# A group norm kernel on one core: longer runs of loads and stores, and more of the sum on TensorE

## The chip, the cores and the metric

The kernel runs on one core of one Trainium2 chip. The metric is the device time of one execution in microseconds (us). A trace of one execution gives the times of each instruction, of each DMA packet, and of each increment that a finished DMA makes on its semaphore.

Engines: PE is TensorE (matmul), DVE is VectorE, ACT is ScalarE, POOL is GpSimd, SP is SyncE, which here only issues the DMAs. A letter q behind a name (SPq) is the engine's sequencer. L129 is line 129 of the kernel.

## The reference

`x` has the shape (128, 1024, 32, 16) in bf16. Each sample has 32 groups of 32 channels; a group is normalized by its own mean and variance, then each channel is scaled and shifted.

```python
def reference(x, g, b):
    xr = x.reshape(B, 32, C // 32, H, W)
    mu = xr.mean(axis=(2, 3, 4), keepdims=True)
    var = ((xr - mu) ** 2).mean(axis=(2, 3, 4), keepdims=True)
    xn = (xr - mu) / jnp.sqrt(var + 1e-5)
    return xn.reshape(B, C, H, W) * g[None, :, None, None] + b[None, :, None, None]
```

## The kernel before

Four samples make a tile: 128 partitions (sample, group) of F = 16384 columns, 4 MB. There are NT = 32 tiles and a ring of 6 slots. A tile is loaded, normalized in place and stored from the same slot.

```python
SLOTS = 6
RUNS = (2, 3, 3, 3, 3, 3, 3, 3, 3, 6)   # stores issued in a row; then as many loads
NQ = 4
PE_CHUNKS = 12                          # chunks of 512 columns that TensorE sums
PAIRED = F - PE_CHUNKS * MM_FREE        # columns that VectorE sums
# ... cut ...
    def store_parts(i):
        return NQ if i == NT - 1 else 1         # the last store in quarters

    def on_sync(e):
        def load(j):
            if j >= SLOTS:
                e.wait_ge(st[j % SLOTS], 16 * (j // SLOTS))     # slot stored?
            e.dma_start(out=slot(j), in_=x_v[j]).then_inc(ld[j % SLOTS], 16)

        def store(i):
            w = F // store_parts(i)
            for p in range(store_parts(i)):
                e.wait_ge(done, NQ * i + NQ // store_parts(i) * (p + 1))
                e.dma_start(out=..., in_=...).then_inc(st[...] or s_fin, 16)

        for j in range(SLOTS):
            load(j)
        i = 0
        for run in RUNS:
            for n in range(run):
                store(i + n)
            i += run
            for j in range(i + SLOTS - run, min(i + SLOTS, NT)):
                load(j)
        e.wait_ge(s_fin, 16 * sum(store_parts(i) for i in range(NT - SLOTS, NT)))
```

For the mean of a tile TensorE adds 12 chunks through an identity matrix into PSUM, and VectorE adds the other 10240 columns as pairs of 5120 (`pair`, tile name jp). ScalarE then reads the mean (jm), takes the squares in two halves (ja), and the standard deviation. VectorE applies 32 `tensor_scalar` instructions to the tile, one per channel (tile name ring).

## Time and profile before

| | before |
|---|---|
| time, median of 3 runs | 632.13 us (631.5 to 632.31) |
| bytes moved | 268.4 MB, half in, half out |
| DMA queue busy | 99.1% of 16 engines' span |
| VectorE / ScalarE / TensorE busy | 84% / 80% / 25% |
| a 32 KB packet on one DMA engine | 1.213 us (median) |

From the page of the kernel before: the mean busy share of the 16 DMA engines in 40 equal slices of the span (in tenths), what they moved, and the data queue with packets, MB and share.

```profile
DMA  8999999999999999999999999999999999999996
GB/s 366 432 432 409 434 436 432 432 434 434 428 432 432 432 434 430 434 430 432 432 432 428 432 432 432 432 432 432 432 432 432 432 426 432 430 430 436 432 421 271
...
q1 hardware_dynamic: 9648, 268.44, 99.1%
```

The rate is flat: most slices are at 428 to 436 GB/s, with the queue busy 99.1%. So the bytes set the time, and what can still be won lies at the start and in the last slice with its 271 GB/s.

The end in stretches of 2 us (kernel before). The columns are: from and to, length, busy time and count of PE, PEld, DVE, ACT and POOL, granted PE clock, mean busy share of the 16 DMA engines, GB/s.

```profile
620.00:622.00 2.00, 0.00 (x0) 0.00 (x0) 0.22 (x1) 0.00 (x0) 0.00 (x0) 0.50 1.09 455
622.00:624.00 2.00, 0.00 (x0) 0.00 (x0) 0.00 (x0) 0.00 (x0) 0.00 (x0) 0.50 0.95 397
624.00:626.00 2.00, 0.00 (x0) 0.00 (x0) 0.00 (x0) 0.00 (x0) 0.00 (x0) 0.50 0.35 147
626.00:628.00 2.00, 0.00 (x0) 0.00 (x0) 0.00 (x0) 0.00 (x0) 0.00 (x0) 0.50 0.19 82
628.00:630.00 2.00, 0.00 (x0) 0.00 (x0) 0.00 (x0) 0.00 (x0) 0.00 (x0) 0.50 0.04 16
```

Read the share as a number of engines: one engine alone is 1/16 = 0.06. All engines are busy until 624 us; then 0.35 (five or six engines), 0.19 (three), and the last packet ends at 628.9 us. The computation was over at 620.2. So the kernel ends some 5 us after most DMA engines are through, because a few of them are late.

How late each one is can be read all along. The trace before has 16 separate increments for each of its 69 DMAs (1104 in all). I read them as the landings of the 16 engines' shares. The spread of a DMA's 16 landings is how far the last engine is behind the first; below it is called the lag. The kernel before, in us; "2nd" is the lag of the last but one:

```
DMA (first landing)   load 12.8   load 51.6   load 207.3   load 333.3   load 449.4   load 565.7   store 604.3
lag of the last          0.78        0.79         2.44         3.58         4.25         5.16        5.45
lag of the 2nd           0.44        0.45         1.40         3.27         4.09         4.98        5.22
```

The groups of the computation that the change touches (kernel before): line, engine, operation, tiles, shapes, count | busy us, mean ns | idle before, and who ended it.

```profile
L287 DVE TENSOR_SCALAR ring<-ring,scl,bia x1024 | 333.7, 413 | 1.2
L254 DVE SCALAR_TENSOR_TENSOR jp<-ring 128x5120 fp8e5 (+1 forms) x32 | 175.8, 5493 | 60.7 <-PE ps L178 48.7 <-issue 12.0
L178 PE MATMUL ps<-ring,eye 128*128 128x512 bf16 x384 | 156.5, 581 | 424.9 <-DVE jp L254 292.5 <-DMA ring<-in_x_dram 132.5
```

And a piece of the timeline in the first 200 us, when six tiles lie ready and compute runs back to back (start, length, engine, line, operation):

```profile
105.14 0.20 DVE L275 RECIPROCAL rstd<-std 128x1 f32 x1
...
106.03 10.43 DVE L287 TENSOR_SCALAR ring<-ring,scl,bia  x32
...
116.96 5.49 DVE L254 SCALAR_TENSOR_TENSOR jp<-ring 128x5120 fp8e5 x1 [0.50 <-issue]
...
122.38 0.20 DVE L275 RECIPROCAL rstd<-std 128x1 f32 x1
```

From one reciprocal to the next is 17.24 us, and VectorE does not rest. The first loads land 9.71 us apart (12.77 and 22.48 us), so a tile's load and store take 2 x 9.7 = 19.4 us of DMA, and in the long run compute, at 17.24 us, is the quicker of the two.

### The profile page before, as it was taken

Reading aid. Unit: us, or ns where it says so; the run is one execution under the profiler, and the core shown is the slowest. Engines: PE = TensorE matmul, PEld = TensorE weight load, DVE = VectorE, ACT = ScalarE, POOL = GpSimd, SP = SyncE. Lnnn points to the kernel's source line nnn. Section 1 sums busy time; section 2 is a strip of 40 time slices with the busy share of each in tenths; the row PEclk is TensorE's granted clock in tenths of the full one; section 3 lists DMA queues with packets and bytes.
Section 4 is the critical chain, followed back from the end, with each engine's and each line's share of the span. In section 5 each row is a group of like instructions: output and inputs, shape, how many; then the busy total and the mean of one; then the engine's idle time right before and its main releaser. Section 6 shows DMA issues by size and latency. Waiting matters only on the chain.

```text
span 630.7 us, 2595 instructions
## 1 busy us (share of the span) xinstructions
PE 156.7 (25%) x385; PEld 0.2 (0%) x2; DVE 529.6 (84%) x1185; ACT 504.0 (80%) x258; POOL 1.0 (0%) x8
## 2 busy tenths in 40 slices
PE   1433333212223220332053014202220430053000
PEld 0000000000000000000000000000000000000000
DVE  1669999999999999699789959995998699599963
ACT  0798999999999999689948977894999499859960
POOL 0000000000000000000000000000000000000000
PEclk9766655566665765666566557656665665565555
DMA  8999999999999999999999999999999999999996
GB/s 366 432 432 409 434 436 432 432 434 434 428 432 432 432 434 430 434 430 432 432 432 428 432 432 432 432 432 432 432 432 432 432 426 432 430 430 436 432 421 271
DMA packets 9745, 268.45 MB, mean 426 GB/s; under 512 B 1168, under 2 KB 1168, under 8 KB 1168
## 3 DMA queue, kind: packets, MB, share of 16 engines
q1 hardware_dynamic: 9648, 268.44, 99.1%
q10 hardware_dynamic: 96, 0.00, 0.0%
q14 instruction: 1, 0.01, 0.0%
HBM read 134.22 MB, written 134.22 MB: 426 GB/s over the span
## 4 chain that ended last, share of the span: by engine, by line
DMA 44%; ACT 40%; DVE 7%; issue 4%; PE 2%; DVEq 2%; SPq 0%
ACT ja L224 37%; DMA out_dram<-ring 28%; DMA ring<-in_x_dram 16%; DVE ring L287 6%; PE ps L178 2%; ACT jm L216 2%; DVEq L270 1%; ACT var L234 1%; ACT std L238 1%; DVE jp L254 1%; DVEq L273 0%; DVE bia L281 0%; DVE scl L277 0%; DVEq L275 0%; DVEq L254 0%
## 5 line engine op out<-in xcount | busy, mean ns | idle before, releaser
L224 ACT ACTIVATE ja<-ring,nm 128x8192 fp8e5<-128x8192 bf16 x64 | 455.8, 7122 | 2.1
L287 DVE TENSOR_SCALAR ring<-ring,scl,bia x1024 | 333.7, 413 | 1.2
L178 PE MATMUL ps<-ring,eye 128*128 128x512 bf16 x384 | 156.5, 581 | 424.9 <-DVE jp L254 292.5
L254 DVE SCALAR_TENSOR_TENSOR jp<-ring 128x5120 fp8e5 (+1 forms) x32 | 175.8, 5493 | 60.7 <-PE ps L178 48.7
L216 ACT ACTIVATE jm<-ps 128x513 fp8e5<-128x513 f32 x32 | 19.2, 602 | 98.7 <-PE ps L178 98.7
L275 DVE RECIPROCAL rstd<-std 128x1 f32 x32 | 6.3, 198 | 11.9 <-ACT std L238 11.9
L224 ACT ACTIVATION_READ_ACCUMULATOR ja<-ring,nm 128x1 f32 x64 | 11.9, 186 | 0.0
L281 DVE SCALAR_TENSOR_TENSOR bia<-scl,nm,gb 128x32 f32<-128x32 f32 x32 | 8.0, 251 | 4.2
L238 ACT ACTIVATE std<-sq,var 128x1 f32<-128x1 f32 x32 | 9.4, 294 | 1.0
L234 ACT ACTIVATE var<-sq,eps_t 128x1 f32<-128x1 f32 x32 | 9.4, 294 | 1.0
L266 DVE COPY gb<-gb_p 128x64 f32<-128x64 f32 x1 | 0.2, 225 | 11.5 <-PE gb_p L173 11.5
L277 DVE TENSOR_SCALAR scl<-gb,rstd 128x32 f32<-128x32 f32 x32 | 7.7, 241 | 1.1
L216 ACT ACTIVATION_READ_ACCUMULATOR jm<-ps 128x1 f32 x32 | 6.2, 194 | 0.0
L254 DVE DVE_READ_ACCUMULATOR jp<-ring (+1 forms) x32 | 4.5, 142 | 0.0
L173 PE MATMUL gb_p<-gb_b,rep 32*128 32x64 bf16 x1 | 0.2, 205 | 11.3 <-DMA gb_b<-in_b_dram 11.3
L212 ACT ACT_TABLE_LOAD x1 | 1.3, 1283 | 1.9 <-issue 1.9
L155 POOL TENSOR_SCALAR_AFFINE_SELECT rep<-ones_b 32x128 bf16<-32x128 bf16 x1 | 0.3, 303 | 0.0
L151 POOL TENSOR_SCALAR_AFFINE_SELECT eye<-ones_b 128x128 bf16<-128x128 bf16 x1 | 0.3, 293 | 0.4 <-issue 0.4
L212 ACT ACTIVATE warm<-eps_t 128x1 f32<-128x1 f32 x1 | 0.2, 203 | 0.0
L145 POOL MEMSET ones_b<- 128x128 bf16 x1 | 0.2, 205 | 0.5 <-SPq L294 0.5
L175 PEld LDWEIGHTS <-eye 128*128 128x128 bf16 x1 | 0.1, 105 | 0.1
L173 PEld LDWEIGHTS gb_p<-gb_b,rep 32*128 32x128 bf16 x1 | 0.1, 100 | 11.3 <-issue 11.3
(5 smaller groups left out, 0.5 us busy)
## 6 DMA issues: line engine op xcount, KB each, us to landing
ring<-in_x_dram SPq DMA_DIRECT2D x32, 4096.0 KB, 29.1
out_dram<-ring SPq DMA_DIRECT2D x31, 4096.0 KB, 31.3
out_dram<-ring SPq DMA_DIRECT2D x4, 1024.0 KB, 7.0
gb_b<-in_g_dram ACTq DMA_DIRECT2D x1, 2.0 KB, 6.5
gb_b<-in_b_dram ACTq DMA_DIRECT2D x1, 2.0 KB, 9.7
```

The source lines that it names most:

```text
L178: return e.add_instruction(mybir.InstMatmult(name=nc.get_next_instruction_name(), engine=e.engine, start_tensor_calc=(k == 0), stop_tensor ...
L212: e.activation(out=warm[:], in_=eps_t[:], func=ACT.Sqrt)
L216: e.activation(out=jm[:], in_=sums_and_pairs(c), func=ACT.Identity, scale=-inv_n, accum_out=nm[:, c : c + 1], saturate=False,).then_inc(me ...
L224: e.activation(out=ja[:], in_=slot(c)[:, h * (F // 2) : (h + 1) * (F // 2)], func=ACT.Square, bias=nm[:, c : c + 1], scale=1.0, accum_out= ...
L234: e.activation(out=var[:], in_=sq[:, 0:1], func=ACT.Identity, bias=eps_t[:], scale=inv_n).then_inc(varred[c], 1)
L238: e.activation(out=std[:, c : c + 1], in_=sq[:, 1:2], func=ACT.Sqrt, bias=var[:], scale=inv_n).then_inc(stded, 1)
L254: e.scalar_tensor_tensor(out=jp[:], in0=part(i, lo, n), scalar=1.0, in1=part(i, lo + n, n), op0=ALU.mult, op1=ALU.add, accum_out=ps[:, bas ...
L270: e.drain()
L275: e.reciprocal(out=rstd[:], in_=std[:, bass.ds(i % SLOTS, 1)]).then_inc(inverted, 1)
L277: e.tensor_scalar(out=scl[:], in0=gb[:, 0:KC], scalar1=rstd[:], scalar2=None, op0=ALU.mult).then_inc(scaled, 1)
L281: e.scalar_tensor_tensor(out=bia[:], in0=scl[:], scalar=nm[:, bass.ds(i % SLOTS, 1)], in1=gb[:, KC : 2 * KC], op0=ALU.mult, op1=ALU.add,). ...
L287: ts = e.tensor_scalar(out=a, in0=a, scalar1=scl[:, k : k + 1], scalar2=bia[:, k : k + 1], op0=ALU.mult, op1=ALU.add,)
```

## The change

Its intent: longer runs, so that the DMA queue changes between loads and stores less often (eight runs instead of ten). Longer runs need tiles earlier, so VectorE's share of the sum is cut by a fifth and given to TensorE, and the third store goes in halves, since its second half is not ready when the queue would run dry. Last, a semaphore increment is put behind the final wait.

```diff
-RUNS = (2, 3, 3, 3, 3, 3, 3, 3, 3, 6)
+RUNS = (3, 4, 4, 4, 4, 4, 3, 6)
-PE_CHUNKS = 12
+PE_CHUNKS = 16
 # ... cut ...
     def store_parts(i):
-        return NQ if i == NT - 1 else 1
+        return {2: 2, NT - 1: NQ}.get(i, 1)
 # ... cut ...
             if j >= SLOTS:
-                e.wait_ge(st[j % SLOTS], 16 * (j // SLOTS))
+                e.wait_ge(
+                    st[j % SLOTS], 16 * sum(store_parts(i) for i in range(j % SLOTS, j, SLOTS))
+                )
 # ... cut ...
         e.wait_ge(s_fin, 16 * sum(store_parts(i) for i in range(NT - SLOTS, NT)))
+        e.sem_inc(s_end, 1)
```

More of the change, by code (lines that the diff above doesn't have):

```diff
@@ L102 @@
     first_in, paired, stded, done = (sem(n) for n in ("first", "pair", "std", "done"))
-    s_gb, s_ones, s_eye, s_gbp, s_fin = (
-        sem(n) for n in ("gbl", "ones", "eye", "gbp", "fin")
+    s_gb, s_ones, s_eye, s_gbp, s_fin, s_end = (
+        sem(n) for n in ("gbl", "ones", "eye", "gbp", "fin", "end")
     )
     def store_parts(i):
-        return NQ if i == NT - 1 else 1
+        return {2: 2, NT - 1: NQ}.get(i, 1)
     def slot(i):
```

## The prediction

The trace before shows one clear dip, 360 GB/s from 58 to 62 us, and the slices at the other nine changes are at 426 to 432. The sum came to 632.1 - 0.9 = 631.2 us; item 1 is its only term. The 0.43 us of a matmul in item 2 is that of the trace before (12 in 5.17 us at 53.62 us).

> What bounds the kernel now. Each tile is 4 MB in and 4 MB out, 268.4 MB in all. The page's slices show 430 to 436 GB/s almost everywhere; the queue table has the DMA engines busy 99.1%. [...] So DMA is the limit, though the chain that ended last names ACT for 40%. In the packet records a 32 KB packet takes 1.213 us (median); 512 per engine are 621.1 us, from the first packet at 2.0. That ends at 623.1. Most of the 16 engines do end near 624, but the last at 628.9, without a gap before: they lag. [...] First-to-last spread of one DMA's 16 landings: 0.8 us for the first load, 1.25 after the first change from loads to stores, 3.1 at 275 us, 5.0 at 507, 5.45 at 604. It grows almost only where stores follow loads (ten times: 60, 100, 158, 217, 275, 333, 391, 449, 507, 565 us), 0.44 us each on average[...]. That lag is the tail: the last slice moves 271 GB/s.
>
> What the change does.
> 1. Eight runs, not ten: two load-to-store changes fewer. Estimate: 2 x 0.44 = 0.9 us less lag on the last engine, directly on the critical path. This is the main term.
> 2. VectorE pairs 4096 columns rather than 5120: at 5.49 us for 5120, about 4.40, so 1.1 us less per tile. Where compute runs back to back (52 to 219 us in the chain) the period is 17.24 us and VectorE never rests; I expect about 16.5, as ScalarE's 15.8 to 15.9 plus hand-over then also limits. TensorE gets 4 x 0.43 = 1.7 us more per tile, hidden, except behind a fresh load. DMA needs 19.4 us per tile, so this buys nothing in the middle; it permits longer runs. I reckon tile 2's first half ready at 75 us (the queue empties at about 81) and tile 6 at 146.5, the queue empty at about 149; with 17.24 per tile it would be 151. A short shortage starves only the leading engines, which have over 4 us in hand.
> 3. Tile 31 is finished about 3 us earlier (now 620.2), and the leading engines' gap of 0.2 to 0.4 us at 604 goes. Neither touches the lagging engines: no gain.
> 4. Store 2 in halves: 16 KB packets. From 8 KB packets (0.309 us, 1.236 per 32 KB) under 0.1 us.
> 5. The last wait is now carried by a branch at 629.35, next instruction 0.155 us later. On an increment: within 0.1 us either way.
>
> Sum: 632.1 - 0.9 = 631.2 us; range 630.2 to 632.1. Chances: faster by over 2% 0.005, within 2% 0.985, slower 0.01.
>
> What would show it. Landing spread at the last whole-tile stores about 4.5 us, not 5.45; last packet about 628, leading engines still near 624; [...]pairing about 4.4 us; period about 16.5; no gap near 149 us; tile 31 done near 617.
>
> What would make it wrong. The growth may depend on bytes, or on how far apart the engines already are, not on the number of changes: then nothing is gained. Longer runs may make each change dearer. Tile 6 may come later than 149 us by more than the lag, and the whole queue stops. The before runs scatter by 0.8 us, about the size of the effect.

## The result

| | before | after |
|---|---|---|
| time, median of 4 runs each | 632.22 us (631.5 to 632.48) | 632.59 us (632.04 to 633.41) |
| ratio, fast runs | | 1.0009 (95%: 0.9991 to 1.0026) |
| instructions in the trace | 2595 | 2719 |
| tile 31 finished | 620.2 us | 617.4 us |
| last packet ends | 628.89 us | 628.91 us |
| lag at the last whole store | 5.45 us | 5.21 us |
| lag of the 2nd there | 5.22 us | 0.66 us |

A ratio is the mean time of one kernel's fast runs over that of the other's of the same rounds, so it is not quite the ratio of the medians quoted. The two kernels can't be told apart. The forecast of 0.9 us less did not come, and 632.59 us lies outside the range.

The page of the kernel after, same lines:

```profile
DMA  8999999999999999999999999999999999999995
GB/s 366 432 432 422 434 428 438 434 434 432 432 432 432 432 430 432 432 432 432 432 432 432 430 432 432 432 432 432 432 432 432 432 434 434 436 424 436 434 423 243
```

The end of the kernel after, in the same stretches:

```profile
620.00:622.00 2.00, 0.00 (x0) 0.00 (x0) 0.00 (x0) 0.00 (x0) 0.00 (x0) 0.50 1.03 434
622.00:624.00 2.00, 0.00 (x0) 0.00 (x0) 0.00 (x0) 0.00 (x0) 0.00 (x0) 0.50 0.92 389
624.00:626.00 2.00, 0.00 (x0) 0.00 (x0) 0.00 (x0) 0.00 (x0) 0.00 (x0) 0.50 0.09 37
626.00:628.00 2.00, 0.00 (x0) 0.00 (x0) 0.00 (x0) 0.00 (x0) 0.00 (x0) 0.50 0.07 29
628.00:630.00 2.00, 0.00 (x0) 0.00 (x0) 0.00 (x0) 0.00 (x0) 0.00 (x0) 0.50 0.02 8
```

This is the surprise. Where 0.35 and 0.19 stood, there is now 0.09 and 0.07: one engine of the sixteen. Fifteen engines are through together, and one still ends at 628.9 us. In this trace the lags of all but one engine stay at about 0.7 us or less up to the last whole store, and that one is as late as before. Its landings show how it gets there: the lag of the last engine (us) at the load just before and just behind each run of stores, with the loads' first landings.

```
run of stores           129-159         207-237         285-314         362-392         440-469         517-537
load before, lag      120.2  0.57     197.6  1.56     275.1  2.81     352.7  3.27     430.3  3.79     507.7  4.35
load behind, lag      168.5  1.33     246.0  2.21     323.5  3.38     401.2  3.81     478.6  4.36     546.4  4.81
```

I had assumed that it jumps where stores follow loads. Two such jumps are there (0.2 us at 198, 0.6 at 275), but the rest is creeping: over every run of four stores it loses 0.5 to 0.8 us (0.46 over the last run, of three), and over most groups of loads nothing.

The computation did what it was meant to do. The groups and the timeline after:

```profile
L290 DVE TENSOR_SCALAR ring<-ring,scl,bia x1024 | 333.7, 420 | 1.2
L181 PE MATMUL ps<-ring,eye 128*128 128x512 bf16 x507 | 185.0, 537 | 393.8 <-DVE jp L257 239.0 <-DMA ring<-in_x_dram 153.6 <-issue 1.1
L257 DVE SCALAR_TENSOR_TENSOR jp<-ring 128x4096 fp8e5 (+1 forms) x32 | 141.6, 4425 | 83.3 <-PE ps L181 71.3 <-issue 12.0
```

```profile
117.70 0.17 DVE L278 RECIPROCAL rstd<-std 128x1 f32 x1
...
118.57 10.43 DVE L290 TENSOR_SCALAR ring<-ring,scl,bia  x32
...
129.49 4.42 DVE L257 SCALAR_TENSOR_TENSOR jp<-ring 128x4096 fp8e5 x1 [0.49 <-issue]
...
134.46 0.16 DVE L278 RECIPROCAL rstd<-std 128x1 f32 x1 [0.48 <-ACT std L241]
```

The pairing takes 4.43 us for 5.49, and the period alternates between 16.16 and 16.77 us (in the second VectorE waits 0.48 us for ScalarE), 16.46 on average for 17.24.

### The profile page after: what moved, and what is told of

The parts are those of the page before. It is cut to its first block, busy times and chain, and to the rows that moved or that the text cites. A ratio compares the mean times of both kernels' runs of the same rounds, so it can differ in the third digit from the quotient of the medians.

```text
span 631.0 us, 2719 instructions
## 1 busy us (share of the span) xinstructions
PE 185.2 (29%) x508; PEld 0.2 (0%) x2; DVE 497.4 (79%) x1185; ACT 504.0 (80%) x258; POOL 1.0 (0%) x8
## 4 chain that ended last, share of the span: by engine, by line
ACT 37%; DMA 23%; DVE 22%; issue 8%; PE 4%; DVEq 3%; SPq 0%; ACTq 0%
ACT ja L227 34%; DMA ring<-in_x_dram 23%; DVE ring L290 20%; PE ps L181 4%; ACT jm L219 2%; DVEq L273 1%; DVEq L276 1%; ACT var L237 1%; DVE jp L257 1%; ACT std L241 1%; DVE bia L284 1%; DVE scl L280 1%; DVEq L257 0%; DVE rstd L278 0%; SPq L131 0%
## 5 line engine op out<-in xcount | busy, mean ns | idle before, releaser
L290 DVE TENSOR_SCALAR ring<-ring,scl,bia x1024 | 333.7, 420 | 1.2
L181 PE MATMUL ps<-ring,eye 128*128 128x512 bf16 x507 | 185.0, 537 | 393.8 <-DVE jp L257 239.0
L257 DVE SCALAR_TENSOR_TENSOR jp<-ring 128x4096 fp8e5 (+1 forms) x32 | 141.6, 4425 | 83.3 <-PE ps L181 71.3
L176 PE MATMUL gb_p<-gb_b,rep 32*128 32x64 bf16 x1 | 0.2, 208 | 11.1 <-DMA gb_b<-in_b_dram 11.1
```

The costliest lines, as they stand in the source:

```text
L181: return e.add_instruction(mybir.InstMatmult(name=nc.get_next_instruction_name(), engine=e.engine, start_tensor_calc=(k == 0), stop_tensor ...
L257: e.scalar_tensor_tensor(out=jp[:], in0=part(i, lo, n), scalar=1.0, in1=part(i, lo + n, n), op0=ALU.mult, op1=ALU.add, accum_out=ps[:, bas ...
L290: ts = e.tensor_scalar(out=a, in0=a, scalar1=scl[:, k : k + 1], scalar2=bia[:, k : k + 1], op0=ALU.mult, op1=ALU.add,)
```

## The experiments

Two theories stood against each other, and a third came up on the way.

- Theory A: one DMA engine loses a little in every store, whatever the runs are. It ends last in both kernels. The changes from loads to stores delay other engines, which in the kernel before happened to end up about as late as that one, so that the trace before could not tell the two causes apart. The change removed, at most, the lateness that did not count.
- Rival B: my prediction, that lateness comes from the changes alone.
- Rival C: the single late engine of the trace after was chance.

About the cause of the creeping: rival D says that the compute engines' traffic in SBUF delays it; theory A1 says that executed instructions do, by themselves.

### b_probe and a_probe: which engine is late

Each kernel with 16 tiny loads queued behind the last store:

```diff
+        for k in range(16, 0, -1):
+            e.dma_start(
+                out=probe[0:k, k * 16 - 16 : k * 16], in_=x_v[0][0:k, 0:16]
+            ).then_inc(s_probe[k - 1], 16)
```

The probe of 5 partitions has 5 landings in the traces, beside one earlier step of its semaphore for the rest of the 16. A late engine is named here by the smallest probe in which its late landing shows, less one: if it shows with 5 partitions and not with 4, it is engine 4. The traces give no numbers of engines, so this is a name; that it stands for one and the same engine in all probes and all runs is my assumption and was not shown.

> The kernel before, with 16 tiny loads queued behind the last store: the k-th names k partitions (k = 16 down to 1)[...]. Theory A (one engine loses about 0.14 us in every 4 MB store, whatever the runs; the changes from loads to stores cost other engines time, but not beyond what that one loses anyway): the last landing is about 5.2 us behind the first, one engine's lag grows by 0.12 to 0.16 us per store inside the runs of stores, some others grow at the changes. Rival B (my prediction: only the changes cost): the late engines lose only at the ten changes, about 0.44 us each.

> The changed kernel with the same 16 probes. Theory A: again exactly one engine 4.5 to 5.5 us late, all others under 1.5 us, and the same engine number as the one in the kernel before whose lag grows in stores. Rival B: the late engine differs from run to run and loses at the eight changes only. Rival C (the single late engine was chance): several engines late, as in the trace before.

Both results were correct (one look each; 634.99 and 634.98 us, with the probes' own time at the end). The latest landing of each probe, in us of the span:

```
partitions    16     15     14     13     12     11     10      9      8      7      6      5      4
b_probe     629.6  629.9  630.1  630.3  630.5  630.7  630.9  631.0  631.2  631.4  631.6  631.8  629.6
a_probe     629.9  630.1  630.2  630.4  630.6  630.8  631.0  631.2  631.4  631.6  631.8  631.9  627.7
```

In both kernels the late landing is there down to 5 partitions (631.8 and 631.9 us) and gone at 4 (629.6 and 627.7): it is engine 4. It was 4.9 us behind in b_probe and 5.0 in a_probe at the last whole store. Its lag grew by 0.35 to 0.42 us over each run of three stores (b_probe, from 159 us on). That supports theory A. What I had expected of a_probe beside it failed: two more engines were 4.0 and 2.5 us late there (engines 13 and 15, named in the same way), and three others in b_probe (15 at 3.4, 14 and 11 at 2.6). So the tidy picture of the trace after was in part chance (a grain of rival C), but engine 4 is the last one in both probed traces and the others come second.

### dma_only: the same bytes without computation

```diff
-        on_gpsimd(nc.gpsimd)
-        on_tensor(nc.tensor)
-        on_scalar(nc.scalar)
-        on_vector(nc.vector)
```

SP issues 32 loads, waits for them, and issues 32 stores (then the probes).

> No computation (a wrong result on purpose): 32 loads into the ring, then 32 stores from it, one change only, then the probes. Theory A: spread of landings stays under 1 us through the loads, grows by about 0.14 us per store after that, in one engine, to about 4.5 to 5 us at the end; time about 2 + 621 + 5 + 2 = 630 us. Rival B (only changes cost): spread under 1.3 us at the end, time about 626 us. Rival D (VectorE or TensorE traffic on SBUF delays that engine): no growth here either, about 626 us.

No engine fell behind: 0.6 us through the loads (the spread of the start), 0.2 us from the first store to the one at 568.6 us. After that one engine was 0.7 to 0.9 us late; that is when SP issued the probes (556 to 588 us), and by the probes it is engine 4 again. The time, 633.25 us, shows no gain: the probes at the end landed up to 629.9 us, and SP waits for all loads before the first store. In dma_tiny, with the same DMAs, the page's slice at that place (304 to 321 us) moved 372 GB/s between slices of 434, by my estimate 16.9 us x (1 - 372/434), some 2.4 us of DMA time. Theory A in its first form is wrong: engine 4 is not slow in stores as such. Something that the computation does makes it slow.

### dma_sbuf and dma_sbuf2: traffic in SBUF without many instructions

```diff
+    def big_v(e):
+        with nc.Fori(0, 11, 1, engines=[e.engine]):
+            for _ in range(10):
+                e.tensor_scalar(out=out_v, in0=src, scalar1=1.0, scalar2=0.0, ...)   # 128 x 8192
+                e.drain()
+    # the same on ScalarE: 80 activations of 128 x 8192
```

Loads and stores go through four slots; VectorE and ScalarE work in the other two. Wrong result on purpose.

> Loads, then stores, through four slots of the ring (a wrong result on purpose), beside some 110 long VectorE and 80 long ScalarE instructions that read and write the other two slots: much traffic in SBUF, few instructions. Rival D: engine 4 falls behind by about 0.14 us per store, 4 to 5 us at the end. Theory A1: under 0.5 us, since there are only about 400 instructions in place of 2600.

The lag stayed at 0.24 us or less to 568.8 us. But VectorE's instructions took 2.29 us each and were over at 273 us, before the stores began, so this said something of ScalarE only. dma_sbuf2 repeats it with VectorE's loop of 130 behind the last load:

> As dma_sbuf, where VectorE had ended before the stores began; here its 130 long instructions (2.3 us each) start with the stores, beside ScalarE's. Rival D (traffic in SBUF delays the late engine): 0.1 us per store or more, 3 us or more behind at 568 us. Theory A1 (executed instructions do): under 0.5 us there.

Two stretches of the stores in dma_sbuf2 (no TensorE here: busy time and count of DVE, ACT and POOL, granted clock, DMA share, GB/s):

```profile
325.00:569.00 244.00, 233.55 (x103) 241.04 (x38) 0.00 (x0) 1.00 1.00 432
569.00:627.00 58.00, 54.46 (x24) 20.09 (x3) 0.00 (x0) 1.00 0.99 425
```

VectorE was busy 96% and ScalarE 99% of the 244 us in which 25 stores ran, more than in the real kernel (84% and 80%), and the lag at 568.5 us was 0.22 us, as without any computation. Rival D is out for these operations (TensorE's reads were not tried).

### dma_tiny: many instructions without traffic

A drain, as written here, names no tile: it has no operand to read or write. The page of dma_tiny counts 7344 instructions.

```diff
+    def tiny(e):                      # on VectorE
+        e.wait_ge(ld[(NT - 1) % SLOTS], ...)     # behind the last load
+        with nc.Fori(0, 400, 1, engines=[e.engine]):
+            for _ in range(16):
+                e.drain()
```

> Loads, then stores, no computation (a wrong result on purpose), and 6400 empty instructions (drains) on VectorE that start with the stores: many instructions, no traffic in SBUF. Theory A1[...]: one engine falls behind by several us while the drains run. Rival D (traffic of the compute engines in SBUF delays it): spread stays under 0.3 us, as without computation.

The lag grew from 0.33 us at the first store to 11.1 at 568.6 us and 14.5 at the last, 0.43 us in each store; every other engine stayed within 0.24 us. By the probes it is engine 4 (on another chip than b_probe and a_probe: 8, not 3). (The kernel's own 677.69 us are the drains', which went on until 675 us.) The end of the DMA in dma_tiny (POOL, clock, DMA share, GB/s):

```profile
325.00:569.00 244.00, 0.00 (x0) 1.00 1.01 431
569.00:627.00 58.00, 0.00 (x0) 1.00 0.99 424
627.00:641.00 14.00, 0.00 (x0) 1.00 0.06 23
```

A share of 0.06 for 14 us is one engine of sixteen, alone. In dma_only nothing moves after 627 us:

```profile
569.00:627.00 58.00, 0.00 (x0) 1.00 0.99 425
627.00:630.00 3.00, 0.00 (x0) 1.00 0.00 0
```

So instructions without operands delay engine 4, and only it (14.5 us, all others within 0.24). More packets of kind "instruction" are not the reason: the pages of dma_tiny and dma_only both count one. Theory A1 is shown for this artificial case.

### drains: the same in the real kernel

```diff
+        tiny(nc.gpsimd)       # 6400 drains on the idle GpSimd, from the first load on
```

The 2.4 ns of this expectation and of the next is an estimate from dma_tiny: 0.43 us per store over some 177 drains per store (6400 drains in about 350 us, 9.7 us a store).

> The changed kernel with 6400 empty instructions (drains) on the idle GpSimd from the first load on. Theory A1 (engine 4 is delayed by about 2.4 ns for each instruction that any engine executes while it stores; from 0.43 us per store at about 177 drains per store): if the drains last about 400 us, half of them meet stores: 3200 x 2.4 ns = 7.7 us more, 640 us, ratio 1.012, engine 4 alone some 13 us behind. If instructions don't matter beside computation: 632.6, ratio 1.000.

641.8 us (641.13 to 642.1), ratio 1.015 (1.0135 to 1.0166), a correct result. The last engine has no probes here and is taken for engine 4. Its lag grew by 1.9 to 2.0 us over each run of four stores between 120 and 352 us, where it grows by 0.55 to 0.65 without drains; over the loads between it stood still (3.70 us at 168 us, 3.67 at 198), and at 608 us it was 9.8. The drains ended at 493 us, but from about 390 us on the lag hardly grew any more: a load waits for all 16 landings of a store, so the other engines ran out of work and waited for engine 4 (the last whole store's first landing came at 608.4 us instead of 604.6). The kernel lost 9 us (641.8 for after_again's 632.77 in the same rounds) to an engine, GpSimd, that had nothing to do with the computation.

### few_instr: fewer instructions in the real kernel

```diff
-            for k, a in enumerate(parts):                      # 32 x 512 columns
+            for q in range(NQ):                                # 4 x 4096 columns
+                k, a = q * KQ, part(i, q * KQ * HW, KQ * HW)
                 ts = e.tensor_scalar(out=a, in0=a, scalar1=scl[:, k : k + 1], ...)
-                if (k + 1) % KQ == 0:
-                    ts.then_inc(done, 1)
+                ts.then_inc(done, 1)
```

> The changed kernel with the normalization in 4 instructions of 4096 columns a tile in place of 32 of 512 (a wrong result on purpose: one channel's factors for eight): 896 instructions fewer, of 2719, the same traffic. Theory A1 (engine 4 loses about 2.4 ns for each instruction executed while it stores): 896 / 2 x 2.4 ns = 1.1 us less lag, about 0.09 us per store where it was 0.13, 3.7 to 4.2 us at the last whole stores; time 631.3 to 631.7 us, ratio to before 0.998 to 0.999. If the lag in the real kernel comes from something else: 0.13 us per store, about 5 us, 632.6 us.

631.19 us (630.59 to 631.52), ratio to before 0.998 (0.9967 to 0.9994): faster by 0.4 to 2.1 us, where 1 us was expected. (The changed kernel was not timed in these rounds; split_only, with the same division of the sums, took 632.54.) The last packet ended at 627.4 us instead of 628.9. The page's first line, and the group of the normalization:

```profile
span 629.5 us, 1823 instructions
```

```profile
L291 DVE TENSOR_SCALAR ring<-ring,scl,bia x128 | 163.7, 1342 | 1.2
```

VectorE's busy time fell too (163.7 for 333.7 us), so the instructions are not the only difference; but in dma_sbuf2, with VectorE busy 96%, the lag stayed at 0.22 us. The lag of the last engine at the last whole store was 3.85 us; the next engine, 3.49.

Put side by side, the lag that the last engine gains in the middle of the kernel:

| kernel | instructions begun per 9.7 us | lag per store, us |
|---|---|---|
| dma_only / dma_sbuf2 | 1 / 13 | 0.00 / 0.00 |
| few_instr | 27 | 0.08 (0.32 to 0.36 per four) |
| b_probe (before's computation) | 40 | 0.13 (0.35 to 0.42 per three) |
| after, after_again | 41 | 0.14 to 0.16 (0.54 to 0.66 per four) |
| drains | 186 | 0.49 (1.94 to 2.04 per four, to 352 us) |
| dma_tiny | 195 | 0.43 |

The first column counts the instructions in the trace in the same stretch. Early stretches are left out in which another engine was last, so few_instr counts from 198 us on and b_probe from 159. By an estimate from the two columns it is roughly 2 to 4 ns for each instruction, and nothing at 13 per store; so it is no strict proportion, but the order is clear.

### runs_of_2: more changes between loads and stores

```diff
-RUNS = (2, 3, 3, 3, 3, 3, 3, 3, 3, 6)
+RUNS = (2, 2, 2, 2, 2, 2, 2, 2, 2, 2, 2, 2, 2, 6)
```

> The kernel before with runs of two (thirteen twos, then six): 14 changes from loads to stores instead of 10, all else as before. Rival B (my prediction, 0.44 us per change on the engine that ends last): 1.8 us slower, 634.0 us, ratio 1.0028. Theory A (engine 4 ends last because it loses about 0.13 us per store; the changes delay other engines, 0.33 us each on the worst): the worst other engine goes from about 3.4 to 4.7 us behind, still in front of engine 4 at 5; time within 0.5 us of before, ratio 0.999 to 1.001.

633.05 us (632.72 to 633.45), ratio 1.0014 (1.0000 to 1.0027). That is 0.9 us, between the two expectations: by this estimate four more changes cost 0.2 us each, half of what I had predicted, but the interval runs from 0 to 1.7 us and so all but reaches both expectations. The trace has the latest two engines at 6.3 and 5.9 us at the last whole store; one of them still grows by 0.1 us per store in the last six (6.00, 6.11, 6.19, 6.29), as engine 4 does, and the other stands still (5.9). So with 14 changes another engine has caught up with the one that ends last; that the changes cost the kernel time is likely, and not clear of the noise.

### split_only, runs_only and after_again: the parts of the change

split_only is the kernel before with 16 chunks on TensorE and the final increment; runs_only is the kernel before with the new runs and the halved third store; after_again is the changed kernel once more.

```diff
 # split_only                                  # runs_only
-PE_CHUNKS = 12                               -RUNS = (2, 3, 3, 3, 3, 3, 3, 3, 3, 6)
+PE_CHUNKS = 16                               +RUNS = (3, 4, 4, 4, 4, 4, 3, 6), store 2 in halves
```

> The kernel before with the new division of the sums (16 chunks on TensorE) and the increment after the last wait; the runs stay ten and the third store whole. Theory A: 632.0 to 632.7 us, ratio 0.999 to 1.001, engine 4 about 5 us behind, no starving: the quicker computation is worth nothing by itself. If it is worth something: below 631.5.

> The kernel before with the new runs and the halved third store alone; the division of the sums between TensorE and VectorE stays (12 chunks). Prediction's reckoning: tile 6 is ready at about 151 us while the leading engines run dry at about 149; they starve 1 to 3 us, and the engine that ends last is only 1 us behind by then, so the end moves by 0.5 to 2 us: 633 to 634.5 us. If the longer runs needed no faster computation: 632.2, ratio 1.000.

> The changed kernel unchanged, for the same chip as the others and as a second trace. Theory A: 632.2 to 632.9 us, ratio 1.000 to 1.001; one engine 4.7 to 5.3 us behind at the last whole stores.

| | us, median of 5 | ratio to before (95%) |
|---|---|---|
| split_only | 632.54 | 1.0003 (0.9989 to 1.0017) |
| runs_only | 635.39 | 1.0047 (1.0033 to 1.0061) |
| after_again | 632.77 | 1.0000 (0.9987 to 1.0014) |

split_only is worth nothing by itself, as expected. The runs alone cost 3 us, a little more than I had reckoned, and where the prediction had put it. SP's own line in runs_only, and the DMA around 149 us:

```profile
150.80 0.33 SPq L131 DMA_DIRECT2D out_dram<-ring  x1
```

```profile
146.00:149.00 3.00, 0.00 (x0) 0.00 (x0) 3.00 (x10) 2.97 (x3) 0.00 (x0) 0.51 0.81 350
149.00:152.00 3.00, 0.00 (x0) 0.00 (x0) 2.50 (x7) 3.00 (x1) 0.00 (x0) 0.50 0.41 175
152.00:155.00 3.00, 0.00 (x0) 0.00 (x0) 3.00 (x1) 3.00 (x1) 0.00 (x0) 0.50 0.83 350
```

And in the kernel after:

```profile
145.78 0.33 SPq L131 DMA_DIRECT2D out_dram<-ring  x1
```

```profile
146.00:149.00 3.00, 0.00 (x0) 0.00 (x0) 2.75 (x1) 3.00 (x1) 0.00 (x0) 0.50 0.96 415
149.00:152.00 3.00, 0.58 (x1) 0.00 (x0) 2.80 (x7) 2.02 (x6) 0.00 (x0) 0.50 1.04 448
152.00:155.00 3.00, 0.00 (x0) 0.00 (x0) 3.00 (x10) 2.97 (x3) 0.00 (x0) 0.50 0.94 404
```

Store 6 closes the second run, and all later loads stand behind it in SP's program. With 12 chunks tile 6 is finished at 150.8 us and the queue has run dry (175 GB/s from 149 to 152); with 16 it is finished at 145.8 and the queue never empties. The faster computation pays for what the longer runs cost; neither lowers what engine 4 loses in stores (split_only, with the faster computation alone, ends its last whole store 5.34 us late). A side remark: in runs_only the pause let the last engine catch up (0.99 us late at 149 us, 0.37 at 172), and its lag at the last whole store was only 3.4 us.

after_again has one engine 5.9 us late at the last whole store, a little more than the 5.3 expected, and all others below 0.5.

### relief15 and tail4: two attempts to unload the late engine

relief15 ran before the probes had named the engine. It stores the first half of tile 16's columns for partitions 0 to 119 and for 120 to 127, then the other half whole. I meant this to take half a store from one engine. Which engines carry these DMAs was not shown; the clauses of the expectation that say it are cut, and its gain of 4 us rested on them: my estimate.

```diff
+            if i == 16:
+                for lo, hi, q0, q1 in ((0, F // 2, 0, 120), (0, F // 2, 120, 128), (F // 2, F, 0, 128)):
+                    e.dma_start(out=o_v[i][q0:q1, lo:hi], in_=slot(i)[q0:q1, lo:hi]).then_inc(...)
```

> The changed kernel; store 16 is split[...]: first half of the columns for partitions 0 to 119[...] and for partitions 120 to 127[...], then the other half for all 128. If the late engine is the highest-numbered one, [...]the end comes about 4 us sooner, 628.5 us, ratio 0.994. If the late engine is another one, no gain, or up to 0.6 us slower. Rival B: no gain, several engines lag by the changes.

642.61 us (642.08 to 642.82), ratio 1.0161 (1.0144 to 1.0178). Nothing was won; the late engine is not the highest by the probes' names, and I had expected a gain for that one alone. What I had not expected is the loss of 10 us (642.61 for before's 632.15) from splitting one store. In the trace the DMA rate sinks when these DMAs run:

```profile
340.00:360.00 20.00, 5.12 (x16) 0.00 (x0) 18.96 (x48) 19.29 (x11) 0.00 (x0) 0.79 1.02 441
360.00:385.00 25.00, 5.97 (x17) 0.00 (x0) 23.28 (x50) 23.53 (x15) 0.00 (x0) 0.64 0.99 360
```

The engines are as busy as ever (0.99) at 360 GB/s for 441: the same busy time moves fewer bytes. The spread of landings jumps from 3 to 13 us there. Why these DMAs are slower, no run here tests.

tail4 issues the last 512 KB of the last store as DMAs of 124 and 4 partitions, at the very end. I meant them for four engines that I took to be idle by then, to spare engine 4. Which engines carry them was not shown, so the clauses that rest on it are cut from the expectation; with them goes its second case, up to 3 us slower if these DMAs were slow as in relief15.

```diff
+                    pieces = [(p * w, at, 0, P), (at, F, 0, 124), (at, F, 124, P)]    # at = F - 2048
```

> The changed kernel; the last half of the last quarter of the last store (512 KB) is issued in DMAs of 124 and 4 partitions[...]. Theory A: [...]1.0 to 1.3 us faster than the changed kernel, 631.4 us. [...]

632.63 us (632.55 to 632.86), against 632.77 for the changed kernel in the same rounds: no gain that can be told from none. The last packet ended at 628.9 us. The landings don't name the engines; but 4 KB packets, 0.16 us each for the most part, took up to 0.66 us between 624 and 627 us, so these DMAs were probably slower than expected. No version came out that beats both kernels and is correct.

## Why the prediction was wrong

The chance given to "within 2%" (0.985) was right; the size was not, and the range missed.

**The step that failed is item 1: "two load-to-store changes fewer. Estimate: 2 x 0.44 = 0.9 us less lag on the last engine, directly on the critical path."** It rests on the sentence "It grows almost only where stores follow loads". For the maximum over the engines, in one trace, this looked true. For the engine that ends last it is false. Take as lag here the last landing less the mean of the eight first. In the trace before, this largest lag gained 0.8 us over the stores and 3.6 from load to load, and in runs_of_2 it gained 0.7 and 4.5: there, by the pace of the first two places, the rank of the latest passes from one engine to another, and the sum hides what each one loses. So I take traces in which one engine is the latest for most of the time; this choice carries part of the argument. In the kernels with ten runs (b_probe, split_only) the last engine gained 2.8 and 3.4 us over the 26 stores that lie between loads, and 1.0 and 0.9 us from load to load, where all its steps at the changes fall. With eight runs (after, after_again, a_probe, tail4) it is 3.5, 3.6, 2.5 and 3.2 us over 27 stores, and 0.7, 1.3, 1.3 and 0.6 from load to load. The part that belongs to the changes is thus about 1 us with ten and about 1 us with eight; the saving of 0.9 us has no room in it. (Early in a trace the last engine is not always the same one, which blurs these sums by some tenths; by runs_of_2 two changes may be worth 0.4 us, an estimate that these times can't confirm.) What counts is the lag over the stores, which the change does not touch. At the last whole store the last engine was 5.45, 4.90 and 5.34 us late with ten runs (before, b_probe, split_only) and 5.21, 5.93, 4.96 and 4.83 with eight (after, after_again, a_probe, tail4): 5.2 on average in both. The change even adds 128 matmuls: 5% more instructions, by an estimate from the table above 5% of 4 us, 0.2 us more lag.

The mistake in reading was to follow a maximum. In the trace before, one engine jumped ahead in lateness at the first changes and stood nearly still between changes, while another crept up behind it by some 0.13 us per store, drew level for the first time at 362 us (3.51 and 3.49 us) and, by its pace, passed it for good only in the last stores (second place: 1.19 us at 169, 1.85 at 236, 2.77 at 314; first place: 2.47, 2.96, 3.23). The landings carry no engine's number, so that the creeping one was engine 4 in that trace too is inferred from its pace. The largest of 16 lags showed the jumps of one and hid the creeping of the other.

Point by point:

- "DMA is the limit": right. The slices show 409 to 438 GB/s in both kernels, nearly all of them 428 or more, between start and end.
- Pairing about 4.40 us, period about 16.5: right (4.43 and 16.46). That this is off the critical path by itself: right (split_only, 1.0003).
- Tile 6 at 146.5 us, the queue empty at about 149, 151 without the faster pairing: right. It was 145.8 and 150.8, and runs_only lost 3 us at that place. The prediction saw that the longer runs need the faster computation, but said that a shortage "starves only the leading engines, which have over 4 us in hand". At 149 us they have 1 us in hand (a lag of 0.97 us in the trace after), not 4; that clause was wrong, and harmless here, since no shortage came.
- Tile 31 about 3 us earlier, without gain: right (617.4 for 620.2 us).
- Halves of store 2 and the last wait, each under 0.1 us: not measured alone; the trace after shows the step behind the last wait 0.1 us shorter (0.06 for 0.155 us), which the time does not show.
- Lag of 4.5 us at the last whole stores, last packet at 628: wrong, 5.2 and 628.9, and 5.9 and 629.3 in after_again.

What stays open is what an executed instruction does to engine 4. It happens in stores and not in loads (drains: 1.9 to 2.0 us over four stores, 3.70 and 3.67 us at the ends of the loads from 168 to 198 us), it needs no operands (dma_tiny: 14.5 us), and drains on VectorE and on GpSimd both do it. By what means it does so, no run here shows. Every timed run here lists its span and granted clock, so each may have been recorded by the profiler; whether an unrecorded execution has the lag can't be told from these runs.

## What to carry to other kernels

When a kernel is bound by DMA, look at the 16 landings of each DMA, not only at the mean share: here the end was set by the latest of 16 (5.21 us behind in the trace after, with the next at 0.66), and so by one engine's history, which the maximum over all at each moment can hide. Before paying for the removal of one cause of delay, check whether another cause ends at the same time; in the trace before, two led to 5 us each, and weakening one of them gave nothing. Longer runs of stores need their last tile finished before the queue runs dry, since all later loads stand behind that store in the issuing engine's program: in runs_only, where that tile came at 150.8 us, the rate fell to 175 GB/s and the kernel took 635.39 us.
